# Thresholded attention and a bilinear FFN: weight conversion steps and the first ffn portions in another order within the opening slots

## The chip, the cores and the metric

One core of a Trainium2 chip runs the whole program. The metric is the device time of one execution in microseconds; several executions are timed, and the median is given. One more execution is recorded by the hardware profiler, which gives the trace that the tables below are read from.

## The reference

Inputs are q, k and v of shape (8, 8, 576, 64) (batch, heads, sequence, head size), a scalar tau, and weights w_a, w_b (512 x 1536) and w_out (1536 x 512) that come as 64-bit floats. For each of the 64 heads:

```
scores = q @ k.T / 8
scores = where(scores >= max(scores, row) - tau, scores, -1e9)
attn   = exp(scores - max);  attn /= sum(attn) + 1e-9
x      = attn @ v            # heads side by side: 4608 x 512
out    = ((x @ w_a) * (x @ w_b)) @ w_out
```

## The kernel before, in words

**Units and slots.** Two heads form a pair (32 pairs). A unit is 128 query rows of both heads of a pair; the last 64 rows of both heads form a shorter one. The main loop (L756) runs over slots g. Slot g issues unit g's scores and weights (mask and softmax), the transposition of the weights of unit g-1, the product with v of a unit some slots back, and a portion of the ffn as a filler. At the end each engine is held to exactly the order in which the code issued its instructions (`keep_order`, L38), so the order of the calls in a slot is the order of each engine's queue.

**One unit.** `scores` (L314): TensorE writes two PSUM tiles `sc`; VectorE takes row maxima `mx` (L332); GpSimd makes `bias` (L334) and `thr` (L336) of them while weights are being converted. `weigh` (L353): ScalarE takes exp (L364), then VectorE's mask (L367) compares with `thr`, multiplies, and sums the row. `reciprocal` (L372) adds 1e-9 to the sums, on ScalarE (L376) or VectorE (L378), and takes the reciprocal on VectorE (L380).

**Two ways to transpose.** For the first eight units (g < BY_PE) ScalarE builds two diagonal matrices of the reciprocals (`diagonals`, L393), and TensorE multiplies the weights by them in the next slot (`turn_pe`, L406 and L412), ScalarE and VectorE copying the result out (L408, L414). Two slots later `weighted_unit` (L499) multiplies by v (L479), ScalarE and VectorE join the two halves (L468, L469), and GpSimd copies the halves crosswise into a second tile `xS` (`exchange`, L489). From unit 8 on ScalarE normalises (L386), VectorE transposes in blocks (L433), and SP's queue writes to DRAM and reads back (L441, L464).

**Weight conversion.** The 64-bit weights come as 36 pieces, each of 128 x 512 numbers as pairs of 32-bit words. `load_weights` (L193) keeps up to four rooms called `raw` filled, and from slot 3 four more in `sums_u32`; a piece's room comes free with its sign step. A piece n of slot g is turned into 32-bit floats in five steps: `convert_first` (two ScalarE instructions, L225 and L226), `convert_clamp` (GpSimd, L232), and in slot g+1 `convert_sign` (VectorE, L238), `convert_shift` (VectorE, L246) and `convert_add` (GpSimd, L251). The table `early` gives slots 0 to 3 two pieces each, slots 4 to 9 three each, slots 10 to 14 two each. The ffn may use a piece only once it is counted in `state["converted"]`.

**The ffn.** `ffn` (L553) is a generator: every step of it issues a few matmuls. For a tile of 128 hidden columns it runs eight steps with w_a (L578), ScalarE copies the product out (L584), then eight with w_b, and VectorE multiplies the two (L586). It gives control back with nothing done (`yield 0, 0, 0`, L566) while the pieces or rows that it needs are missing. `advance` (L699) takes steps until the columns owed are used up:

```
advance((PORTIONS[2] if g > BY_PE else sum(PORTIONS[:3])) * pace)   # L826
advance(PORTIONS[3] * pace)                                         # L827
```

In slots 0 to 8 the whole portion stands at these two lines, at the slot's end; later slots spend parts of it at L787, L799, L826 and L827. The first block of rows exists from slot 5 on, and each of slots 5 to 8 issues 11 or 12 steps.

**PSUM.** Four buffers (`banks`, L125) of two banks each serve scores, turned weights, products and ffn tiles in turn.

**The order in a slot of the start, before:** scores and maxima; join and exchange of the unit two back; signs of all pieces of the slot before, then their shifts, then their adds (the last piece's first); new loads; exp and masks; the transposition of unit g-1; the first steps and clamp of this slot's first piece; add of 1e-9 (on ScalarE) and reciprocal; diagonals; the first steps and clamps of the other pieces; loads; the ffn's portion.

Of the kernel before, what the change touches and what calls it, by code (L numbers as in the profile page):

```python
# [23 lines left out]
BY_PE = 8  # L24
# [8 lines left out]
PORTIONS = (0.3, 0.35, 0.15, 0.2)  # L33
# [18 lines left out]
def kernel(  # L52
# [38 lines left out]
    nc = tc.nc  # L91
# [40 lines left out]
    loaded = {}  # L132
# [38 lines left out]
    for f in range(NG):  # L171
        for c in range(HP):
            for dst, w in ((wa_sb, w_a), (wb_sb, w_b)):
                src = []
                for r in range(2):
                    chunks = [(2 * c + e) % HP * 2 + (r + (c >= HP // 2)) % 2 for e in range(2)]
                    cols = slice(f * CW + r * CH, f * CW + (r + 1) * CH)
                    rows = w[:, cols].bitcast(U32).rearrange("(k p) f -> p k f", p=D)
# [3 lines left out]
        pieces.append((wo_sb[:, F, :], [w_out[F * P:(F + 1) * P, :].bitcast(U32)]))  # L182
    NPIECES = len(pieces)
    raws, stages, extra, taken = {}, {}, [], {}
    state = {"loaded": 0, "converted": 0, "rows": 0, "sums": False, "through": 0, "over": False}


    NSUM = NF // 2 * 3 * CH
# [46 lines left out]
    def convert_sign(n):  # L235
        if n in stages:
            low, hi = stages[n].bitcast(U32), raws.pop(n)[:, :, 1]
            nc.vector.scalar_tensor_tensor(out=low, in0=hi, scalar=0x80000000, in1=low,  # L238
                                           op0=ALU.bitwise_and, op1=ALU.bitwise_or)
            if n in taken:  # L240
                extra.append(taken.pop(n))

    def convert_shift(n):
        if n in stages:
            top = pieces[n][0].bitcast(U32)
            nc.vector.tensor_scalar(top, top, 3, None, op0=ALU.logical_shift_left)  # L246

    def convert_add(n):
        if n in stages:
            top, low = pieces[n][0].bitcast(I32), stages.pop(n).bitcast(I32)  # L250
            nc.gpsimd.tensor_tensor(top, top, low, op=ALU.add)  # L251
            state["converted"] += 1


    scalars = const.tile([P, 8], FP32, name="scalars")
# [55 lines left out]
    def prep_copy(mT, tp):  # L311
        nc.vector.tensor_copy(mT.rearrange("p (c k) -> p c k", c=2), tp)  # L312
# [40 lines left out]
    def weigh(i, u):  # L353

        sc, thr, bias, mx, biased = scored.pop((i, u))
        n = len(sc)
        sums = small.tile([P, 2], FP32, tag="sums", name="sums")
        ws = rooms_of(i, u)
        sb = [s.rearrange("p c (n e) -> p c n e", e=Q) for s in sc]
        wb = [w.rearrange("p (c n) e -> p c n e", c=2) for w in ws]  # L360
        for j in range(n):
            if not biased:
                nc.scalar.activation(bias[:, j:j + 1], mx[:, j:j + 1], AF.Copy, scale=e_nscale)
            nc.scalar.activation(wb[j], sb[j], AF.Exp, bias=bias[:, j:j + 1], scale=e_scale)  # L364
        for j in range(n):
            wv = wb[j]
            nc.vector.scalar_tensor_tensor(  # L367
                out=wv, in0=sb[j], scalar=thr[:, j:j + 1], in1=wv,
                op0=ALU.is_ge, op1=ALU.mult, accum_out=sums[:, j:j + 1])
        weights[i, u] = (ws, sums)  # L370

    def reciprocal(i, u, engine):  # L372
        ws, sums = weights[i, u]
        n = len(ws)
        if engine is nc.scalar:
            nc.scalar.activation(sums[:, 0:n], sums[:, 0:n], AF.Copy, bias=1e-9)  # L376
        else:
            nc.vector.tensor_scalar_add(sums[:, 0:n], sums[:, 0:n], 1e-9)  # L378
        rcp = small.tile([P, 2], FP32, tag="rcp", name="rcp")
        nc.vector.reciprocal(rcp[:, 0:n], sums[:, 0:n])  # L380
        weights[i, u] = (ws, rcp)

    def normalise(i, u):
        ws, rcp = weights[i, u]
        for j, w in enumerate(ws):
            nc.scalar.activation(w, w, AF.Copy, scale=rcp[:, j:j + 1])  # L386
# [35 lines left out]
    def width(i, h):  # L422
        return (HALF, HALF, TAIL)[h] if i < HP else (HALF, HALF + TAIL)[h]
# [269 lines left out]
    def cost():  # L693

        return BLOCK_COLS - (NF // 2 * CH if state["sums"] else 0)
# [3 lines left out]
    def advance(cols):  # L699
        running["owed"] += cols  # L700
        while running["owed"] > 0:
            if running["ffn"] is None:
                if not blocks:
                    running["owed"] = 0.0
                    return
                running["ffn"] = ffn(*blocks.pop(0))
                running["left"] = cost()
            step, rest, whole = next(running["ffn"], (None, 0, 0))
            if step == 0:
                running["owed"] = 0.0  # L710
                return
            if step is None:
                running["ffn"] = None
                state["through"] += 1
            else:
                running["owed"] -= step
                running["left"] -= step
                running["done"] = running["done"] + step if rest else 0
                running["rest"] = rest
                running["room"] = min(ROOM, whole // 2)  # L720
# [9 lines left out]
    def backlog():  # L730
        return len(blocks) * cost() + (running["left"] if running["ffn"] is not None else 0)
# [16 lines left out]
    for name in ("q", "k"):  # L748
        prep_copy(*prep_pe(0, name))
    early = {}  # L750
    n = 0
    for g in range(NPIECES):
        size = min(3 if 4 <= g < 10 else 2, NPIECES - n)
# [1 line left out]
        n += size  # L755
    for g in range(len(units) + PV_LAG):  # L756
        written = len(pending)
        here = g < len(units)
        converting = bool(early.get(g)) or bool(early.get(g - 1))
        if here:  # L760
            i, u = units[g]
            scores(i, u)
        turn_back()
        exchange_blocks()
        pace = (PACE if g > BY_PE else PACE_EARLY) * BLOCK_COLS
        if g > BY_PE:
            pace = min(pace, backlog() / (min([a for a in arrivals if a > g] + [len(units) + PV_LAG + 1]) - g))
        pace += (NSLOT + 1) // 2 * S / (NT + 1) + CATCH_UP * max(backlog() - BLOCK_COLS, 0)
        if 2 <= g < BY_PE + 2:
            weighted_unit(*units[g - 2])  # L770
            running["owed"] -= (NSLOT + 1) // 2 * P
        if g < 3:
            prep_copy(*prep_pe(g + 1, "q"))
        for n in early.get(g - 1, []):
            convert_sign(n)
        for n in early.get(g - 1, []):
            convert_shift(n)
        for n in early.get(g - 1, [])[-1:] + early.get(g - 1, [])[:-1]:
            convert_add(n)
        if g == 3:  # L780
            for c in range(0, NSUM - 2 * CW + 1, 2 * CW):
                extra.append(sums_u32[:, c:c + 2 * CW].rearrange("p (f w) -> p f w", w=2))
        load_weights(RAWS)
        if g > BY_PE and g <= len(units):
            turn_blocks(*units[g - 1])
        if g > BY_PE:
            advance(PORTIONS[0] * pace)  # L787
        if here:
            weigh(i, u)
        if 0 < g <= BY_PE:  # L790
            turn_pe(*units[g - 1])
        if g < 3:
            prep_copy(*prep_pe(g + 1, "k"))
        for p in range(HP, NPR):
            for name, d in (("q", 2), ("k", 1)):
                if g == first[p] - d:
                    prep(p, name)
        if g > BY_PE:
            advance(PORTIONS[1] * pace)  # L799
            n = g - PV_LAG  # L800
            if BY_PE <= n < len(units) and part(*units[n]):
                make_room()
                weighted(*part(*units[n]))
                running["owed"] -= (NSLOT + 1) // 2 * width(*part(*units[n]))
        for n in early.get(g, [])[:1]:
            convert_first(n)
            convert_clamp(n)
        if here:
            reciprocal(i, u, nc.scalar if converting else nc.vector)
        if here and g < BY_PE:  # L810
            diagonals(i, u)
        elif here:
            normalise(i, u)
        for n in early.get(g, [])[1:]:
            convert_first(n)
            convert_clamp(n)
        load_weights(RAWS)
        for p in range(HP, NPR):
            for name, d in (("q", 4), ("k", 3)):
                if g == first[p] - d:  # L820
                    load(p, name)
        for p in range(1, NPR):
            if g == first[p] - 1:
                load_v(p)
        store(written)
        advance((PORTIONS[2] if g > BY_PE else sum(PORTIONS[:3])) * pace)  # L826
        advance(PORTIONS[3] * pace)  # L827

        if not converting and not state["sums"]:
            state["slots"] = state.get("slots", 0) + 1  # L830
            for n in {1: (0,), 2: (1,), 3: (2,)}.get(state["slots"], ()):
                for z in range(2):
                    weight_sums(n, z)
            if state["slots"] >= 3 and state["through"]:
                for z in range(2):
                    weight_sums(3, z)
                state["sums"] = True
# [38 lines left out]
```

## Time and profile before

| | us |
|---|---|
| median of 7 runs | 1482.24 (1478.39 to 1483.79) |
| the profiled execution's own time | 1483.91 |
| its span, first to last instruction | 1482.0 |
| TensorE matmul busy | 1423.6 (96%) |
| VectorE busy | 927.0 (63%) |
| ScalarE busy | 670.4 (45%) |
| GpSimd busy | 361.3 (24%) |

Busy time is the time that an engine's instructions cover; matmuls are pipelined, so a busy TensorE is not one at its peak. The mean granted TensorE clock is 0.995 of full speed. In the tables PE is TensorE's matmul, PEld its weight load, DVE VectorE, ACT ScalarE, POOL GpSimd and SP the engine whose queue issues the DMAs. A row of a timeline gives start, duration, engine, line, operation, output and input, the number of instructions merged, and in brackets the idle time of the engine ahead of it and what ended that. Row sums of idle time by what ended it are called waits.

### The profile page before, as it was taken

How to read it: one execution, taken by the hardware profiler on the slowest of the kernel's cores; microseconds unless marked ns; L12 is line 12 of the kernel's file. 1: busy time of each engine (PE TensorE's matmuls, PEld its weight loads, DVE VectorE, ACT ScalarE, POOL GpSimd, SP SyncE). 2: the span in 40 equal slices, each digit the busy share in tenths (PEclk: the TensorE clock that was granted, in tenths of full speed). 3: DMA queues.
4: the chain of work that ended last, by engine and by line, in shares of the span. 5: the costliest groups of instructions: out<-in, count | busy, mean ns of one | idle time of the engine just before them, and what ended most of it. 6: DMA issues, size and time to landing. Idle time of an engine off the chain costs nothing.

```text
span 1482.0 us, 57127 instructions
## 1 busy us (share of the span) xinstructions
PE 1423.6 (96%) x25344; PEld 1197.3 (81%) x25344; DVE 927.0 (63%) x2068; ACT 670.4 (45%) x1213; POOL 361.3 (24%) x563
## 2 busy tenths in 40 slices
PE   5778999999999999999999999999999999999998
PEld 4667587898779798898888788889888898888886
DVE  5767677778657776776655766577756775622212
ACT  4866355545445554544443544455444454411010
POOL 3876512204030312122121203030404040310000
PEclk9999999999999999999999999999999999999999
DMA  9956888889868876797556876588756986530000
GB/s 202 213 171 168 170 167 182 195 155 191 201 129 182 188 173 151 167 188 170 110 133 132 181 165 150 119 187 180 158 145 135 192 175 158 136 90 16 2 17 16
DMA packets 624582, 220.75 MB, mean 149 GB/s; under 512 B 542928, under 2 KB 612048, under 8 KB 624336
## 3 DMA queue, kind: packets, MB, share of 16 engines
q1 hardware_dynamic: 621968, 216.52, 66.6%
q8 instruction: 199, 3.26, 0.9%
q10 hardware_dynamic: 2368, 0.59, 0.2%
q14 instruction: 47, 0.39, 0.1%
HBM read 127.40 MB, written 89.65 MB: 146 GB/s over the span
## 4 chain that ended last, share of the span: by engine, by line
PE 87%; DVE 5%; DMA 2%; ACT 2%; SPq 1%; issue 1%; POOL 1%; ACTq 0%; DVEq 0%; POOLq 0%
PE pab L578 46%; PE po L621 19%; PE pv L479 10%; PE sc L325 10%; PE po L665 1%; DMA swap<-tw 1%; DVE tw L433 1%; DVE tw L367 1%; DVE mx L332 1%; DVE low L238 1%; ACT tw L364 1%; SPq L151 0%; DMA sums_u<-in_moe_w_a_dram 0%; SPq L206 0%; DMA sums_u<-in_k_dram 0%
## 5 line engine op out<-in xcount | busy, mean ns | idle before, releaser
L332 DVE TENSOR_REDUCE mx<-sc 128x1 f32<-128x576 f32 x288 | 205.3, 750 | 129.3 <-PE sc L325 118.5
L578 PE MATMUL pab<-xS,wa_sb 64*64 64x256 f32 (+1 forms) x3584 | 271.8, 371 | 0.9 <-POOL xS L489 0.9
L578 PE MATMUL pab<-xS,wb_sb 64*64 64x256 f32 (+1 forms) x3584 | 268.0, 372 | 0.2 <-issue 0.2
L325 PE MATMUL sc<-kT,qT 64*64 64x288 f32 x2304 | 242.0, 411 | 21.9 <-DVE kT L312 7.8
L590 POOL TENSOR_TENSOR h<-h 128x256 f32<-128x256 f32 x168 | 117.5, 732 | 543.4 <-PE po L621 540.3
L578 PE MATMUL pab<-xT,wb_sb 64*64 64x256 f32 (+1 forms) x3200 | 236.2, 370 | 5.6 <-DVE h L586 4.1
L578 PE MATMUL pab<-xT,wa_sb 64*64 64x256 f32 (+1 forms) x3200 | 235.8, 368 | 5.3 <-POOL thr L336 2.1
L621 PE MATMUL po<-wo_sb,h 64*64 64x256 f32 x3264 | 240.4, 376 | 0.0
L386 ACT ACTIVATE tw<-tw,rcp 128x576 f32<-128x576 f32 x244 | 176.4, 769 | 131.4 <-DVE rcp L380 131.3
L364 ACT ACTIVATE tw<-sc,bias,scalars 128x576 f32<-128x576 f32 x260 | 214.9, 832 | 41.8 <-POOL bias L334 26.4
L367 DVE SCALAR_TENSOR_TENSOR tw<-sc,thr,tw 128x576 f32<-128x576 f32 x260 | 203.9, 803 | 23.9 <-ACT tw L364 22.9
L578 PEld LDWEIGHTS pab<-xS,wa_sb 64*64 64x64 f32 x3584 | 192.3, 133 | 31.6 <-POOL xS L489 5.2
L578 PEld LDWEIGHTS pab<-xS,wb_sb 64*64 64x64 f32 x3584 | 194.2, 134 | 24.9 <-issue 0.8
L621 PEld LDWEIGHTS po<-wo_sb,h 64*64 64x64 f32 x3264 | 174.7, 132 | 26.3
L578 PEld LDWEIGHTS pab<-xT,wa_sb 64*64 64x64 f32 x3200 | 169.1, 133 | 30.3 <-DVE kept L469 4.3
L578 PEld LDWEIGHTS pab<-xT,wb_sb 64*64 64x64 f32 x3200 | 170.4, 134 | 27.8 <-DVE h L586 4.5
L479 PE MATMUL pv<-wT,vm 64*64 64x320 f32 (+3 forms) x2592 | 185.9, 379 | 5.0 <-ACT h L584 3.2
L325 PEld LDWEIGHTS sc<-kT,qT 64*64 64x64 f32 x2304 | 142.4, 134 | 55.3 <-issue 16.8
L621 PE MATMUL po<-sums_u,h 64*64 64x256 f32 x2448 | 180.8, 376 | 0.0
L433 DVE STREAM_TRANSPOSE tw<-tw 128x576 f32<-128x576 f32 x240 | 171.7, 753 | 0.2 <-ACT tw L386 0.2
L586 DVE TENSOR_TENSOR h<-h,pab 128x512 f32<-128x512 f32 (+1 forms) x112 | 73.4, 656 | 148.8 <-PE pab L578 140.9
L479 PEld LDWEIGHTS pv<-wT,vm 64*64 64x64 f32 x2592 | 140.0, 134 | 28.4 <-ACT h L584 4.3
(85 smaller groups left out, 1238.0 us busy)
## 6 DMA issues: line engine op xcount, KB each, us to landing
swap<-tw SPq DMA_DIRECT2D x240, 288.0 KB, 5.3
wT<-swap SPq DMA_DIRECT2D x28, 1440.0 KB, 7.6
wT<-swap SPq DMA_DIRECT2D x32, 1152.0 KB, 6.4
vm<-in_v_dram SPq DMA_DIRECT2D x32, 288.0 KB, 4.8
qT<-in_q_dram SPq DMA_DIRECT2D x112, 72.0 KB, 3.7
kT<-in_k_dram SPq DMA_DIRECT2D x112, 72.0 KB, 4.5
swap<-wt SPq DMA_DIRECT2D x112, 72.0 KB, 2.8
out_dram<-kept SPq DMA_DIRECT2D x30, 256.0 KB, 4.5
```

The costliest lines, as they stand in the source:

```text
L238: nc.vector.scalar_tensor_tensor(out=low, in0=hi, scalar=0x80000000, in1=low, op0=ALU.bitwise_and, op1=ALU.bitwise_or)
L325: nc.tensor.matmul(sc[j if u < NT else 0][to, c], qT[r, q0:q0 + D], kT[r, c * SH:(c + 1) * SH], start=True, stop=True)
L332: nc.vector.tensor_reduce(mx[:, c], sc[j], axis=AX.XY, op=ALU.max)
L364: nc.scalar.activation(wb[j], sb[j], AF.Exp, bias=bias[:, j:j + 1], scale=e_scale)
L367: nc.vector.scalar_tensor_tensor(out=wv, in0=sb[j], scalar=thr[:, j:j + 1], in1=wv, op0=ALU.is_ge, op1=ALU.mult, accum_out=sums[:, j:j + 1])
L386: nc.scalar.activation(w, w, AF.Copy, scale=rcp[:, j:j + 1])
L433: nc.vector.transpose(w, w)
L479: nc.tensor.matmul(pv[j * D:(j + 1) * D, r], vm[rows, k0], wT[rows, k0], start=(s == (NT if j == r else 0)), stop=(s == NT - 1))
L578: nc.tensor.matmul(pab[c * D:(c + 1) * D, r], w[rows, f // n, k, fs + c * D:fs + (c + 1) * D], moving, start=(k == 0), stop=(k == H - 1))
L586: nc.vector.tensor_tensor(ht, ht, pab, op=ALU.mult)
L590: (nc.vector if state["over"] else nc.gpsimd).tensor_tensor(*a, **kw)
L621: nc.tensor.matmul(po[c * D:(c + 1) * D, r, y], ht[rows, t0:t0 + D], other[rows, f], start=(f == 0), stop=(f == NF // 2 - 1))
```

## The change

- The steps that finish a piece (sign, shift, add) are put together in `convert_rest(g, k)`, which handles piece k of the slot before. Piece 0 stays where all of them were, pieces 1 and 2 follow the reciprocal and the diagonals or the normalising; in slots 0 to 8 the ffn's portion stands between pieces 1 and 2.
- In slots 0 to 7 the add of 1e-9 and the reciprocal directly follow the masks, both on VectorE.
- In slots 0 to 8 the ffn's whole portion is issued ahead of the first steps of this slot's second and third piece. In later slots it stays at the end.
- A piece that is added counts as converted from the start of the next slot on.

```diff
@@ -182,7 +182,7 @@
         pieces.append((wo_sb[:, F, :], [w_out[F * P:(F + 1) * P, :].bitcast(U32)]))
     NPIECES = len(pieces)
     raws, stages, extra, taken = {}, {}, [], {}
-    state = {"loaded": 0, "converted": 0, "rows": 0, "sums": False, "through": 0, "over": False}
+    state = {"loaded": 0, "added": 0, "converted": 0, "rows": 0, "sums": False, "through": 0, "over": False}
 
 
     NSUM = NF // 2 * 3 * CH
@@ -249,7 +249,7 @@
         if n in stages:
             top, low = pieces[n][0].bitcast(I32), stages.pop(n).bitcast(I32)
             nc.gpsimd.tensor_tensor(top, top, low, op=ALU.add)
-            state["converted"] += 1
+            state["added"] += 1
 
 
     scalars = const.tile([P, 8], FP32, name="scalars")
@@ -748,6 +748,14 @@
     for name in ("q", "k"):
         prep_copy(*prep_pe(0, name))
     early = {}
+
+    def convert_rest(g, k):
+
+        for n in early.get(g - 1, [])[k:k + 1]:
+            convert_sign(n)
+            convert_shift(n)
+            convert_add(n)
+
     n = 0
     for g in range(NPIECES):
         size = min(3 if 4 <= g < 10 else 2, NPIECES - n)
@@ -755,6 +763,7 @@
         n += size
     for g in range(len(units) + PV_LAG):
         written = len(pending)
+        state["converted"] = state["added"]
         here = g < len(units)
         converting = bool(early.get(g)) or bool(early.get(g - 1))
         if here:
@@ -771,12 +780,7 @@
             running["owed"] -= (NSLOT + 1) // 2 * P
         if g < 3:
             prep_copy(*prep_pe(g + 1, "q"))
-        for n in early.get(g - 1, []):
-            convert_sign(n)
-        for n in early.get(g - 1, []):
-            convert_shift(n)
-        for n in early.get(g - 1, [])[-1:] + early.get(g - 1, [])[:-1]:
-            convert_add(n)
+        convert_rest(g, 0)
         if g == 3:
             for c in range(0, NSUM - 2 * CW + 1, 2 * CW):
                 extra.append(sums_u32[:, c:c + 2 * CW].rearrange("p (f w) -> p f w", w=2))
@@ -787,6 +791,8 @@
             advance(PORTIONS[0] * pace)
         if here:
             weigh(i, u)
+        if here and g < BY_PE:
+            reciprocal(i, u, nc.vector)
         if 0 < g <= BY_PE:
             turn_pe(*units[g - 1])
         if g < 3:
@@ -805,12 +811,15 @@
         for n in early.get(g, [])[:1]:
             convert_first(n)
             convert_clamp(n)
-        if here:
-            reciprocal(i, u, nc.scalar if converting else nc.vector)
         if here and g < BY_PE:
             diagonals(i, u)
         elif here:
+            reciprocal(i, u, nc.scalar if converting else nc.vector)
             normalise(i, u)
+        convert_rest(g, 1)
+        if g <= BY_PE:
+            advance(pace)
+        convert_rest(g, 2)
         for n in early.get(g, [])[1:]:
             convert_first(n)
             convert_clamp(n)
@@ -823,8 +832,9 @@
             if g == first[p] - 1:
                 load_v(p)
         store(written)
-        advance((PORTIONS[2] if g > BY_PE else sum(PORTIONS[:3])) * pace)
-        advance(PORTIONS[3] * pace)
+        if g > BY_PE:
+            advance(PORTIONS[2] * pace)
+            advance(PORTIONS[3] * pace)
 
         if not converting and not state["sums"]:
             state["slots"] = state.get("slots", 0) + 1
```

## The prediction

> **What bounds the kernel now.** I read the page's busy row first, then busy time by stretches, then the engines' timelines from 40 to 110 us, then the waits of PE. The busy row says PE 96%, which hides where its idle time lies. So I cut the span at the starts of slots 0, 4, 10 and 16 (a slot starts with its first score matmul: 11.25, 40.21, 101.72, 154.08 us); columns are PE, PEld, DVE, ACT, POOL, clock, DMA share, GB/s:
>
> ```profile
> 11.25:40.21 28.96, 22.11 (x233) 16.68 (x233) 21.97 (x48) 19.03 (x38) 15.11 (x27) 1.00 1.03 196
> 40.21:101.72 61.51, 44.02 (x940) 37.85 (x942) 41.55 (x99) 45.64 (x91) 49.87 (x67) 0.97 0.79 198
> 101.72:154.08 52.36, 42.85 (x942) 36.49 (x938) 42.01 (x87) 33.35 (x58) 35.92 (x43) 0.97 0.67 165
> 154.08:200.00 45.92, 44.98 (x623) 30.67 (x619) 28.36 (x62) 18.37 (x31) 20.52 (x27) 0.96 0.85 172
> 200.00:1482.00 1282.00, 1267.50 (x22617) 1073.73 (x22609) 791.15 (x1769) 552.76 (x998) 239.21 (x394) 1.00 0.66 144
> ```
>
> From 154 us on PE idles 15.4 us in 1328: it sets the end, and whatever the first 16 slots save or lose moves the end by as much. Those slots hold 33.9 us of idle PE (6.85 + 17.5 + 9.5), and all of the change lies in them. In slots 4 to 9 POOL is the busiest engine (49.87 of 61.5), in 10 to 15 PE and DVE. One slot's chain, slot 8 into 9:
>
> ```profile
> 81.64 0.30 POOL L336 TENSOR_SCALAR thr<-mx,scalars 128x2 f32<-128x2 f32 x1
> 82.32 1.32 POOL L489 COPY xS<-xT 64x128 f32<-64x128 f32 x2 [0.39 <-DVE xT L469]
> 85.34 2.53 POOL L251 TENSOR_TENSOR wb_sb<-wb_sb,low 128x512 int32<-128x512 int32 x2 [1.70 <-DVE wb_sb L246]
> 87.82 1.28 POOL L251 TENSOR_TENSOR wa_sb<-wa_sb,low 128x512 int32<-128x512 int32 x1
> ...
> 90.95 0.55 POOL L334 TENSOR_SCALAR bias<-mx,scalars 128x1 f32<-128x1 f32 x2
> ```
> ```profile
> 90.18 0.65 ACT L226 ACTIVATE low<-raw 128x512 f32<-128x512 uint32 x1
> 90.74 0.35 ACT L584 COPY h<-pab 128x256 f32<-128x256 f32 x1
> ```
> ```profile
> 91.14 1.20 PE L479 MATMUL pv<-wT,vm 64*64 64x128 f32 x34 [1.60 <-ACT h L584]
> ...
> 97.83 1.99 PE L578 MATMUL pab<-xT,wb_sb 64*64 64x128 f32 x32 [2.68 <-DVE h L586]
> 99.58 1.88 PE L578 MATMUL pab<-xS,wb_sb 64*64 64x128 f32 x32
> ```
>
> The reader is to see three things. POOL waits 1.70 us, because its first add comes after all three signs and shifts on DVE. The softmax bias of the next slot stands behind POOL's adds and clamps. And ACT's copy of a finished ffn product stands behind four conversions, though PE had that product ready at about 87.3; PE's next matmul lacks the PSUM buffer meanwhile.
>
> **The change, part by part.** Slots 0 to 3. In slot 2 the two signs and two shifts fill DVE from 30.26 to 32.23, ahead of the masks (L367) and of the k copy (L312) that slot 3's scores wait for. The second pair, 0.98, now follows that copy and lies in the 1.22 us in which DVE waits for the next scores. The add (0.28, L378) and reciprocal (0.17) come ahead of the copy: +0.45. Net -0.53 in slots 1 and 2, +0.45 in slot 0, which has no pair to finish. Slot 3 ends with ACT's turn copies; its bias now waits for the late add and clamp (pair done about 1.0 after the scores start, 1.25 + 0.6 more; bias at 2.8 instead of 2.1): +0.6. Sum 0.0.
>
> SP's queue: a piece's room is freed by its sign. Counting rooms (four raw, four sums, the latter from slot 3), piece 5 loads only after the sign that now ends slot 1, at about 27.5 instead of 23.61; 1.25 us of issue and 5.6 of landing (the median; 9.7 the longest) bring it to 34.4, and ACT takes it at about 34.5 (35.35 before). Piece 7 likewise: 42.3 against 42.24. Cover gone: 0 to 4 us, I take +0.5. The v loads queued behind have a slot to spare. From slot 4 on loads run 8 us or more ahead.
>
> Slots 4 to 8. Three PE waits end with the late copy (L584): 1.63 at 60.11, 0.86 at 79.29, 1.60 at 91.14. The copy now precedes the four conversions (4 x 0.56), so these 4.1 us go. The conversions wait for PE's ffn instead, but the tile is done within 0.1 us of the diagonals in my walk. What is late next is POOL: from bias to bias its slots took 9.27, 9.83, 9.73, 10.49 and 12.82 us (slots 5 to 9, 52.14 in all). Unhindered it needs 0.55 + 0.30 + 0.7 to 1.3 + 3 x 1.25 + 3 x 0.6 = 7.1 to 7.7. I walked slots 5 to 9 in the new order with these durations: the first add follows the exchange at once, since one sign and shift (0.98) fit beside it; the second follows the pair behind the masks; the third follows a pair behind DVE's ffn product. Slot 5, from its first bias: DVE's join ends at 0.5, pair 1 at 1.5, the masks (exp has just finished) at 2.95, add and reciprocal at 3.45, turn copy at 3.75, pair 2 at 4.75, pair 3 at 5.7. POOL: bias and thr, which the first sign holds, to 1.45; exchange 2.15; add 1 to 3.4; clamp 1 to 4.05; add 2 from 4.75 to 6.0; add 3 to 7.25; two clamps to 8.45, the next bias. The five slots so: 8.5, 8.7, 9.6 (add 3 waits 0.8 for the ffn product), 9.1, 9.3, mean 9.0.
>
> The moved pairs then run beside adds, which no row shows. Nearest rows: the exchange took 1.32 beside signs (82.32) and 0.62 beside masks (45.99), so about half speed; and thr took 1.54 beside signs (71.79), 0.30 without. For a pair beside an add that is 0 to 0.98; I take 0.5 by the exchange, the nearer form, in four of five slots: mean 9.4. Gain 5 x (10.4 - 9.4) = 5.1; with slot 4, where one pair leaves the masks' front, 5.5. Ends: 3.6 (both pairs stop POOL, 9.7 a slot) and 13.6 (7.7 a slot).
>
> [...]
>
> Slot 9. At 97.83 PE waits 2.68 for a product behind three pairs and two transposes, then issues 64 matmuls in 3.5 us, where 104.00 and 104.88 took 1.75. Two pairs (1.96) leave the front. The wait is in POOL's period already; of the slow stretch's 1.7 us I take 1.0, bounds 0 and 1.7.
>
> [...]
>
> Slots 10 to 15. Order there changes on DVE and POOL alone. PE waits ended by DVE: 1.53 (109.25), 1.38 (116.63), 3.71 (144.94), 0.96 (152.25). One pair less ahead (two in slot 10) takes at most 1.53 + 0.98 + 0.98 + 0.96 = 4.45. The second add now starts a pair behind the reciprocal, and the bias of the next slot stands behind it: reciprocal + 1.1 + 1.25 + 0.6 = 3.0 against 2.8 by normalise, conversion and clamp. 0.2 x 5 = 1.0 lost. Net -3.5.
>
> Held pieces. A piece counts one slot later. Slot 7's ffn then has 14 pieces and needs 16: it stops after 9 of 11 k-steps, and 2 x 0.22 = +0.45 comes later, on a full PE. Later gates have pieces to spare (by counting steps, 34 in slot 15, where output begins).
>
> Sum: 0.0 + 0.5 - 5.5 - 1.0 - 3.5 + 0.45 = -9.05. The profiled execution took 1483.91 (span 1482.0 and 1.9 around it), 1.67 over the median of the seven runs, 1482.24. So 1474.9 on the profiled one's scale, and **1473** on the median's.
>
> **Rivals.** (1) Part of it is taken back: POOL is stopped by the pairs and the loads of slots 2 and 3 come late. Then slots 4 to 8 give 3.6, slots 10 to 15 half (1.7), the slow stretch stays, loads cost 2: -5.3 + 2 + 0.45 = -2.9, 1479.3. For it: thr's 1.54. Against: the exchange. (2) Slower: POOL's in-order queue. The last add waits for a sign behind DVE's ffn product, which waits for PE; product, pair, add and two clamps (0.35 + 0.98 + 1.25 + 1.2 = 3.8) then stand between PE's last ffn matmul and the next bias. Place: slots 5 to 15. It decides as soon as bias to bias exceeds the 10.4 of now; with two adds held up so (5.05) against 3.8 a slot has 1.25 more than my 9.4 and ends at 10.65 before any stop of POOL; 0.5 for that makes it 11.15, +0.7 in 11 slots, less the 2 us that earlier copies still give: +6, 1488. For it: my slot 7 already has POOL waiting 1.4 us this way. Against: the ffn of slots 5, 6 and 8 completes no second-weight tile late in the slot. (3) More than forecast: PE keeps pace with 7.7 us of POOL work; the 13.6 end less 3 for the waits that stay, with 1.7 and 4.45, and the +0.95 of loads and held steps: -16, 1466. (4) It does not act: buffers are handed out otherwise, PE waits for a mask instead of a copy: 1482.
>
> **How the numbers follow.** Forecast 0.60 (1468 to 1478), (1) 0.17, (2) 0.10, (3) 0.08, (4) 0.05. The range must leave out 0.2 at most: it reaches from 1466 over forecast and (1) to 1481, leaving out (2), (4) and the outer part of (3). 0.2% is 3 us, about what a measurement here can tell from no change. Faster by more: forecast, (3) and half of (1), 0.77. Within: half of (1) and (4), 0.13. Slower: 0.10.
>
> **What would show it.** Right: no PE wait on ACT's h copy in slots 5 to 9; POOL's bias-to-bias near 9.4; the idle before the first add gone from 1.70 to under 0.5; slot 10's scores 7 us earlier; slot 16's 9 earlier; from there on the same lengths. Wrong: adds above 1.7 us beside signs, bias more than 4 us behind its scores, an ACT wait on a weight load in slots 2 and 3, or the gain of slot 16 missing at the end, which would mean that PE doesn't set it.

## The result and the profile after

The changed kernel takes 1475.84 us (median of 22 runs, 1472.35 to 1481.24) against 1482.33 of before in the same comparison: ratio 0.9961, 95% interval 0.9952 to 0.9970, so 5.8 us less (4.4 to 7.1; the two medians lie 6.5 apart). Its profiled execution took 1476.51 (span 1474.5), 7.4 less than that of before (1483.91). The forecast was 1473.

These are the stretches of the changed kernel, cut at its own starts of slots 0, 4, 10 and 16, with the columns of the prediction's first fence:

```profile
10.95:39.40 28.45, 22.13 (x233) 17.03 (x233) 22.70 (x49) 18.08 (x34) 14.87 (x27) 1.00 1.06 198
39.40:97.07 57.67, 44.73 (x933) 39.08 (x935) 49.24 (x100) 43.14 (x84) 46.10 (x65) 0.94 0.82 195
97.07:148.91 51.84, 44.03 (x958) 37.39 (x954) 45.68 (x89) 34.49 (x60) 34.04 (x44) 0.97 0.75 191
148.91:194.80 45.89, 43.59 (x612) 29.75 (x608) 27.34 (x62) 18.30 (x30) 21.72 (x28) 0.99 0.82 168
194.80:1474.50 1279.70, 1265.20 (x22618) 1088.67 (x22609) 792.41 (x1771) 551.97 (x998) 238.59 (x394) 1.00 0.66 144
```

Slots 4 to 9 are 3.8 us shorter (61.51 to 57.67), and DVE now has more busy time there than POOL: 49.24, where it had 41.55. It runs about as many rows (x100 for x99); some of them take longer (the four shifts of slots 0 to 15 that meet an add of GpSimd take 1.50 each, without an add 0.42 is the median). Slots 10 to 15 lost 0.5 us (52.36 to 51.84), slots 0 to 3 0.5.

The same chain as in the prediction, slot 8 into 9, on GpSimd:

```profile
83.18 0.63 POOL L489 COPY xS<-xT 64x128 f32<-64x128 f32 x2
83.90 1.28 POOL L251 TENSOR_TENSOR wb_sb<-wb_sb,low 128x512 int32<-128x512 int32 x1
...
87.58 1.65 POOL L251 TENSOR_TENSOR wa_sb<-wa_sb,low 128x512 int32<-128x512 int32 x1 [1.17 <-DVE wa_sb L246]
89.60 1.29 POOL L251 TENSOR_TENSOR wb_sb<-wb_sb,low 128x512 int32<-128x512 int32 x1 [0.37 <-DVE wb_sb L246]
...
92.03 1.23 POOL L334 TENSOR_SCALAR bias<-mx,scalars 128x1 f32<-128x1 f32 x2
```

ScalarE, where the copy of the ffn product (L584) now stands ahead of four conversions:

```profile
88.10 0.37 ACT L584 COPY h<-pab 128x256 f32<-128x256 f32 x1
88.37 0.68 ACT L225 ACTIVATE wb_sb<-sums_u 128x512 f32<-128x512 f32 x1
```

TensorE, slots 8 and 9:

```profile
84.44 1.91 PE L578 MATMUL pab<-xT,wa_sb 64*64 64x128 f32 x32 [2.92 <-DVE tw L367]
...
89.74 1.14 PE L479 MATMUL pv<-wT,vm 64*64 64x128 f32 x33
...
95.05 1.10 PE L578 MATMUL pab<-xT,wb_sb 64*64 64x128 f32 x32 [1.33 <-DVE tw L367]
```

The reader is to see that each wait which the change was to remove is gone: the first add follows the exchange at once (the 1.70 has no successor), and the product with v no longer waits 1.60 for ScalarE (89.74 has no bracket). But GpSimd now waits 1.17 and 0.37 between its adds, and from bias to bias it still takes 9.89 (82.14 to 92.03). TensorE waits for VectorE's masks instead, 2.92 us, because the bias comes late: 5.3 us behind the scores of slot 8, where it was 3.2. One such wait stands in each of slots 5 to 8 (0.78, 1.59, 1.58 and 2.92 us); before, no wait there was ended by the masks.

### The profile page after: what moved, and what is told of

It is laid out like the page before. It is cut to its first block, busy times and chain, and to the rows that moved or that the text cites. A ratio compares the mean times of both kernels' runs of the same rounds, so it can differ in the third digit from the quotient of the medians.

```text
span 1474.5 us, 57127 instructions
## 1 busy us (share of the span) xinstructions
PE 1421.8 (96%) x25344; PEld 1213.8 (82%) x25344; DVE 939.4 (64%) x2076; ACT 667.3 (45%) x1205; POOL 356.0 (24%) x563
## 4 chain that ended last, share of the span: by engine, by line
PE 85%; DVE 6%; DMA 3%; ACT 2%; SPq 2%; issue 2%; POOL 1%; DVEq 0%; ACTq 0%; POOLq 0%
PE pab L578 46%; PE po L621 19%; PE sc L325 10%; PE pv L479 9%; DVE mx L332 1%; DVE tw L367 1%; DMA swap<-tw 1%; DVE low L238 1%; SPq L143 1%; DVE tw L433 1%; PE po L665 1%; DMA raw<-in_moe_w_a_dram 0%; ACT tw L364 0%; DMA sums_u<-in_moe_w_a_dram 0%; SPq L441 0%
## 5 line engine op out<-in xcount | busy, mean ns | idle before, releaser
L621 PEld LDWEIGHTS po<-wo_sb,h 64*64 64x64 f32 x3264 | 177.9, 132 | 23.4
L578 PEld LDWEIGHTS pab<-xT,wb_sb 64*64 64x64 f32 x3200 | 172.1, 133 | 24.8 <-DVE h L586 3.2
L325 PEld LDWEIGHTS sc<-kT,qT 64*64 64x64 f32 x2304 | 145.8, 134 | 50.7 <-issue 15.7
L479 PEld LDWEIGHTS pv<-wT,vm 64*64 64x64 f32 x2592 | 144.1, 134 | 22.6 <-DVE h L586 2.8
```

Source lines behind the costliest of these rows:

```text
L325: nc.tensor.matmul(sc[j if u < NT else 0][to, c], qT[r, q0:q0 + D], kT[r, c * SH:(c + 1) * SH], start=True, stop=True)
L479: nc.tensor.matmul(pv[j * D:(j + 1) * D, r], vm[rows, k0], wT[rows, k0], start=(s == (NT if j == r else 0)), stop=(s == NT - 1))
L578: nc.tensor.matmul(pab[c * D:(c + 1) * D, r], w[rows, f // n, k, fs + c * D:fs + (c + 1) * D], moving, start=(k == 0), stop=(k == H - 1))
L621: nc.tensor.matmul(po[c * D:(c + 1) * D, r, y], ht[rows, t0:t0 + D], other[rows, f], start=(f == 0), stop=(f == NF // 2 - 1))
```

## The experiments

Each ratio is to the kernel before, run on the same chip in the same comparison. "us" is the ratio times 1482. Lengths of stretches come from one profiled execution of each kernel.

| kernel | ratio (95%) | us | slots 0-3 | 4-8 | 9 | 10-11 | 12-14 | 15 |
|---|---|---|---|---|---|---|---|---|
| before | 1 | 0 | 28.96 | 48.13 | 13.38 | 18.24 | 24.98 | 9.14 |
| changed | 0.9961 (0.9952 to 0.9970) | -5.8 | 28.45 | 49.37 | 8.30 | 19.53 | 22.05 | 10.26 |
| changed_again | 0.9962 (0.9945 to 0.9979) | -5.6 | 28.16 | 48.02 | 9.81 | 21.24 | 22.26 | 10.26 |
| split_only | 0.9998 (0.9986 to 1.0011) | -0.3 | 29.17 | 49.85 | 11.24 | 21.70 | 22.81 | 8.85 |
| ffn_ahead_only | 0.9986 (0.9972 to 1.0001) | -2.1 | 30.54 | 48.38 | 9.95 | 18.66 | 24.96 | 9.56 |
| sums_early_only | 1.0076 (1.0060 to 1.0093) | +11.3 | 36.33 | 52.39 | 12.89 | 18.52 | 24.95 | 10.00 |
| count_later_only | 0.9971 (0.9959 to 0.9984) | -4.3 | 28.96 | 46.34 | 12.96 | 18.37 | 22.31 | 9.19 |
| hold_1 | 0.9977 (0.9964 to 0.9990) | -3.4 | 28.39 | 50.99 | 13.36 | 18.02 | 22.32 | 10.75 |
| hold_4 | 0.9985 (0.9974 to 0.9997) | -2.2 | 32.37 | 46.61 | 11.48 | 20.52 | 23.37 | 9.40 |
| count_and_ffn | 0.9935 (0.9917 to 0.9952) | -9.6 | 32.86 | 48.67 | 10.07 | 18.36 | 22.34 | 9.18 |
| no_sums_early | 0.9965 (0.9952 to 0.9979) | -5.2 | 27.70 | 51.20 | 8.37 | 20.62 | 22.47 | 8.89 |
| no_split | 0.9998 (0.9987 to 1.0008) | -0.3 | 34.95 | 46.11 | 14.24 | 19.02 | 22.30 | 9.78 |
| early_rcp_no_add | 0.9965 (0.9950 to 0.9980) | -5.2 | 29.41 | 47.87 | 13.09 | 18.01 | 22.29 | 10.74 |
| pairs_together | 0.9958 (0.9942 to 0.9973) | -6.2 | 28.09 | 48.83 | 8.20 | 19.30 | 22.72 | 10.02 |

One caution for the table: slots 0 to 3 of before, hold_4 and hold_1 are the same program and took 28.96, 32.37 and 28.39 us in their one profile each, so a difference of 3 or 4 us there carries nothing by itself. Slots 12 to 14 repeat to 0.05 us among the kernels without the split that share TensorE's order there; the two profiles of the changed kernel differ by 0.21.

### The four parts alone

Each of these four is the kernel before with one part of the change.

**split_only.** Pieces 1 and 2 are finished behind the diagonals or the normalising.

```diff
-        for n in early.get(g - 1, []):
-            convert_sign(n)
...
+        convert_rest(g, 0)
...
+        convert_rest(g, 1)
+        convert_rest(g, 2)
```

> The kernel before with one part of the change: pairs of sign and shift (and their add) of pieces 1 and 2 behind the reciprocal; ffn portion, reciprocal and counting as before. Theory A (the gain is slot 9, where fewer pairs stand ahead of DVE's ffn product, and pairs beside adds gain nothing in slots 4 to 8): faster by 4 to 6 us, slot 9 shorter than 9.5 us (13.4 before), bias to bias of slots 5 to 8 within 0.4 of before's 9.8. Theory B (the gain is the early ffn copy): within 2 us of before, slot 9 above 12 us.

Measured: 0.9998, no difference. The time is as theory B expected, but slot 9 took 11.24, which neither theory allows (under 9.5, above 12), so neither is shown by this run.

**ffn_ahead_only.** In slots 0 to 8 the ffn's portion goes ahead of the late conversions.

```diff
+        if g <= BY_PE:
+            advance(pace)
         for n in early.get(g, [])[1:]:
             convert_first(n)
```

> The kernel before with one part of the change: in slots 0 to 8 the ffn portion ahead of the first steps of pieces 1 and 2; all signs, shifts and adds in front as before. Theory A: faster by at most 3 us, since POOL's ring sets slots 5 to 8, whoever is early on PE. Theory B: faster by 4 to 7 us, the three waits of PE on the copy (4.1 us) gone and slot 9 shorter by over 2 us.

Measured: 0.9986, 2.1 us less, with an interval that just takes in no change. Slot 9 falls from 13.38 to 9.95. The time keeps to theory A's bound of 3 us, and theory B's 4 to 7 us did not come, though slot 9 shrank as B asked.

**sums_early_only.** Add and reciprocal at once behind the masks in slots 0 to 7.

```diff
+        if here and g < BY_PE:
+            reciprocal(i, u, nc.vector)
         if 0 < g <= BY_PE:
             turn_pe(*units[g - 1])
```

> The kernel before with one part of the change: in slots 0 to 7 the add of 1e-9 and the reciprocal on VectorE right behind the masks. Theory A and B: no change, within 1 us; 0.45 us more on VectorE in slot 0, 1 and 2 ahead of the k copy, less wait of the diagonals. A third theory (this part carries the gain by freeing ScalarE): faster by over 3 us.

Measured: 11.3 us slower, the largest effect of any part, and against the change; none of the three theories expected it. VectorE and then GpSimd of this kernel just behind the masks of slot 1, and what TensorE does next:

```profile
25.86 1.11 DVE L378 TENSOR_SCALAR sums<-sums 128x2 f32<-128x2 f32 x1
27.00 0.17 DVE L380 RECIPROCAL rcp<-sums 128x2 f32<-128x2 f32 x1
```
```profile
25.65 1.28 POOL L251 TENSOR_TENSOR wa_sb<-wa_sb,low 128x512 int32<-128x512 int32 x1
```
```profile
28.07 2.21 PE L325 MATMUL sc<-kT,qT 64*64 64x288 f32 x16 [1.39 <-DVE kT L312]
```

An addition on two numbers a row takes 1.11 us and ends at 26.97, 0.04 behind the end of GpSimd's add at 26.93. With no add of GpSimd under way it takes 0.17 to 0.28 (five of the eight in the changed kernel). The copy of k stands behind it, and the next scores behind that; they then run at half pace (2.21 instead of 1.22). This adds to the loss: from 23 us to the start of slot 10 the granted clock is at half for 24.8 us in this profile, and for 3.4 us in that of before.

**count_later_only.** A piece counts as converted one slot later.

```diff
-            state["converted"] += 1
+            state["added"] += 1
...
+        state["converted"] = state["added"]
```

> The kernel before with one part of the change: a piece counts from the next slot on, so that two ffn k-steps of slot 7 come in slot 8 and TensorE's whole later order moves by two steps. By the prediction's term: 0.45 us slower at most. Rival: the other order of TensorE behind slot 16 is what gave the changed kernel 2.3 us there; then faster by 1.5 to 3 us, most of it behind 160 us.

Measured: 0.9971, 4.3 us less. The part that the forecast booked as a loss of 0.45 is the largest gain of the four. The rival expected 1.5 to 3 us, most of it behind 160 us; the gain is larger, and what the profile shows of it lies ahead of slot 16 (see below).

### Parts together, and parts left out

**count_and_ffn** joins later counting and the ffn ahead, without split and early sums.

```diff
+        state["converted"] = state["added"]
...
+        if g <= BY_PE:
+            advance(pace)
         for n in early.get(g, [])[1:]:
             convert_first(n)
```

> The kernel before with two parts: the later counting and the ffn portion ahead of the late conversions; no split, reciprocal as before. If the parts add up: 4.3 + 2 = 6 us faster than before, as much as the whole change, which then owes nothing to the split and the early sums. Rival (both remove the same waits of slots 8 and 9): 4 us or less.

Measured: 1472.35 against 1481.67, 0.9935. It beats both kernels: 9.6 us less than before, and by medians about 3.5 less than the changed one (the two intervals only touch, that of changed_again overlaps, and they were not run on one chip). It is more than the 6 us expected if the parts add up, and the rival's 4 us or less is refuted.

**no_sums_early** is the changed kernel with the reciprocal back in its old place.

```diff
-        if here and g < BY_PE:
-            reciprocal(i, u, nc.vector)
...
+        if here:
+            reciprocal(i, u, nc.scalar if converting else nc.vector)
```

> The changed kernel without one part: the add of 1e-9 (on ScalarE again) and the reciprocal stand where they stood. Theory L (VectorE's short add waits for a GpSimd add that runs beside it; in the changed kernel the split has moved GpSimd's adds away, so that the early sums cost little there): within 1.5 us of the changed kernel, 5 to 8 us faster than before. Rival (the early sums carry some of the change's gain, their own loss being of the old order alone): 2 us or more slower than the changed kernel, under 4.5 us faster than before.

**no_split** is the changed kernel with all pairs ahead of the masks again.

```diff
-        convert_rest(g, 0)
+        for n in early.get(g - 1, []):
+            convert_sign(n)
...
-        convert_rest(g, 1)
...
-        convert_rest(g, 2)
```

> The changed kernel without one part: all signs, shifts and adds in front again, early sums, early ffn and later counting kept. Theory L: VectorE's add of 1e-9 stands beside GpSimd's second add again and takes 1.1 us instead of 0.3 in slots 1 to 3, TensorE goes to half pace there; slot 4 starts 5 to 8 us later than in the changed kernel, the whole is 3 to 8 us slower than before. Rival (early sums alone lost time for some other reason that the other parts remove): faster than before by 3 us or more.

Measured, on the chip of count_and_ffn: 0.9965 and 0.9998. The first keeps to theory L. The second does not: L expected 3 to 8 us slower than before, and it is as fast as before, though its slots 0 to 3 are 6.5 us longer than the changed kernel's, as L asked (5 to 8). So neither part gains by itself. Without early sums the split costs 4.4 us (0.9965 against 0.9935, intervals that touch; on before alone it costs nothing, 0.9998); with them it saves 5.5 (0.9961 against 0.9998, on different chips). What the rows show for the saving is that it moves GpSimd's second add away from the small addition, which takes 0.17 to 0.45 in the changed kernel and 1.11 to 1.27 in five of its seven meetings in no_split; in the other two GpSimd's add was nearly over (0.30 and 0.44). In sums_early_only, where the addition has the same place, it takes 1.11 to 1.27 in five of seven too, and 0.29 and 0.44 in the others. Early sums without the split cost 9.3 (0.9998 against 0.9935). The two together are repair and damage.

### Is it the lock, or the early reciprocal?

"Lock" means here that an instruction of VectorE is not over until an add of GpSimd, which runs beside it, is over, as with the addition above (26.97 behind 26.93).

**early_rcp_no_add** is count_and_ffn with the reciprocal of slots 0 to 7 at once behind the masks, and without the addition of 1e-9 in these slots.

```diff
-        if engine is nc.scalar:
+        if engine is None:
+            pass
+        elif engine is nc.scalar:
...
+        if here and g < BY_PE:
+            reciprocal(i, u, None)
```

> The kernel before with the later counting and the ffn part ahead of the late conversions, and with the reciprocal of slots 0 to 7 on VectorE at once behind the masks, but without the addition of 1e-9 (left out in those slots). Pairs of converting steps stay together as before. Theory of the lock (the small addition waits out GpSimd's addition, 1.11 us against 0.17 to 0.28 alone; the reciprocal itself is not the price): 8 to 12 us faster than before, like the later counting and the ffn part alone (0.9935). Rival (any small instruction on VectorE ahead of the copies of turned weights is held up, or the reciprocal is locked out as the addition was): within 2 us of before, like the changed kernel without the split (0.9998), with the reciprocal of slots 2 and 3 at 0.8 us or more.

Measured: 0.9965, between the two. VectorE, GpSimd and TensorE in the same place as above:

```profile
26.39 0.17 DVE L382 RECIPROCAL rcp<-sums 128x2 f32<-128x2 f32 x1
```
```profile
26.21 1.27 POOL L251 TENSOR_TENSOR wa_sb<-wa_sb,low 128x512 int32<-128x512 int32 x1
```
```profile
27.46 1.22 PE L325 MATMUL sc<-kT,qT 64*64 64x288 f32 x16 [1.02 <-DVE kT L312]
```

The reciprocal runs beside the add at its usual 0.17 in all seven meetings of slots 1 to 7, these scores keep full pace, and slots 0 to 3 take 29.41, where the two kernels with the addition in this place take 36.33 and 34.95 (count_and_ffn, with neither, took 32.86 in its one profile). By these ratios the addition costs 4.9 us of the 9.3 (0.9998 to 0.9965; two chips, but the intervals lie apart). The other 4.4 (0.9965 to 0.9935, different chips, intervals that just overlap) is not explained. In the one profile slot 9 is 3.0 us longer than in count_and_ffn, of which 1.6 is half pace behind a wait of the same 3.08; the rest stays open. The forecast of 8 to 12 for the lock was too high, the rival's "within 2 us of before" is refuted.

### What sets GpSimd's period?

**pairs_together** is the changed kernel with pieces 1 and 2 both signed and shifted ahead of the ffn's portion, and then both added.

```diff
-        for n in early.get(g - 1, [])[k:k + 1]:
+        some = early.get(g - 1, [])[0:1] if k == 0 else early.get(g - 1, [])[1:]
+        for n in some:
             convert_sign(n)
+        for n in some:
             convert_shift(n)
+        for n in some:
             convert_add(n)
...
-        convert_rest(g, 2)
```

> The changed kernel with the signs and shifts of the second and third piece together behind the diagonals, ahead of the ffn part, and GpSimd's two additions behind them. Theory of the lock (GpSimd's last addition waits 0.97 for a pair that itself waited for the addition before it): the 0.97 before the last addition goes, bias to bias on GpSimd falls from 10.14 to 9.7 or less in slots 4 to 9, and the time is 0 to 3 us below the changed kernel's. Rival (the period is set elsewhere, by VectorE's masks and copies): bias to bias stays at 10.0 or more and the time within 1 us of the changed kernel's, or above it where VectorE's copies stand behind the pairs.

Measured: 0.9958, beside 0.9962 of the changed kernel on the same chip: no difference. GpSimd's last two adds of slot 8 and the next bias:

```profile
87.61 1.39 POOL L251 TENSOR_TENSOR wa_sb<-wa_sb,low 128x512 int32<-128x512 int32 x1 [1.76 <-DVE wa_sb L246]
88.96 1.28 POOL L251 TENSOR_TENSOR wb_sb<-wb_sb,low 128x512 int32<-128x512 int32 x1
...
91.38 1.23 POOL L334 TENSOR_SCALAR bias<-mx,scalars 128x1 f32<-128x1 f32 x2
```

The wait between the two adds is gone as expected, and is paid ahead of the first of them (1.76 for 1.17). From 51.83 to 102.04 the mean of five periods is 10.04 us; the changed kernel has 10.14, and 10.20 in its second profile. The theory expected 9.7 or less, so it falls for this question, and the rival holds. What the profile shows instead is a ring through three engines. In slot 7 of this kernel the bias starts at 71.39, the masks end at 74.46, both pairs at 77.60, both adds at 79.98, two clamps at 81.7, and the next bias starts there. In either order pairs 2 and 3 stand between the masks, which need the bias, and the adds, which the next bias stands behind.

Three pairs of kernels differ by the split alone; without it all pairs stand ahead of the masks. The mean of the three periods from the bias of slot 5 to that of slot 8 is 9.61 us in before and 10.62 in split_only, 9.78 in count_and_ffn and 10.71 in no_sums_early, 9.66 in no_split and 10.07 in changed (10.20 in its second profile). So the split lengthens the period by 0.4 to 1.0 us. That it does so by closing this ring was read off the traces; no run tests it.

### Why does later counting gain?

**hold_4** and **hold_1** are the kernel before with four contraction steps, or one, less of the ffn owed in slot 7.

```diff
+        if g == 7:
+            running["owed"] -= 4 * P
```

> The kernel before with the ffn of slot 7 cut by four k-steps (512 columns less are owed), which come later; nothing else. Theory P (the later counting gains by where the ffn's tiles then end in the slots, not by holding steps): anything between 3 us faster and 4 us slower. Rival (fewer ffn steps in slot 7 are what gains): 4 to 9 us faster.

> The kernel before with one contraction step less of the ffn part owed in slot 7, and nothing else; TensorE's order becomes that of the later counting but for some twenty instructions. Theory of alignment (what the later counting won is that slot 7 no longer ends on a half-open tile of the ffn that keeps one of four PSUM buffers): 3 to 5 us faster than before. Rival (the later counting wins by something else, or holding any work does it): within 1.5 us of before, as with four steps less (0.9985).

Measured: 0.9985 and 0.9977. Holding four steps gives 2.2 us, within theory P's range and short of the rival's 4 to 9. Holding one gives 3.4, as much as the later counting within the intervals and within the 3 to 5 that were expected. But the place that I named for it was wrong, so that number came out by luck. In hold_1 slot 7 still ends on an open tile, and slot 8's scores still wait for the buffer:

```profile
76.04 0.40 PE L578 MATMUL pab<-xT,wa_sb 64*64 64x128 f32 x8
76.26 1.14 PE L325 MATMUL sc<-kT,qT 64*64 64x288 f32 x8
78.58 0.70 PE L325 MATMUL sc<-kT,qT 64*64 64x288 f32 x4 [1.19 <-ACT h L584]
...
144.11 1.22 PE L325 MATMUL sc<-kT,qT 64*64 64x288 f32 x16 [0.82 <-DVE tw L367]
```

(This profiled execution took 1482.41, five over the kernel's median, with slots 8 and 9 partly at half pace, 16 matmuls of L406 in 3.79 at 82.58 where the changed kernel has 2.05; its stretches 4 to 8 and 9 are not used.) What hold_1 and the later counting share is the order of TensorE's work from slot 9 on, and with it slots 12 to 14: 22.32 and 22.31 us. The same three slots take 22.34, 22.30 and 22.29 in the three other kernels with that order and without the split, and 24.98, 24.96 and 24.95 in before, ffn_ahead_only and sums_early_only. That is 2.65 us, the same in eight profiles. TensorE at the end of slots 12 and 14, in before:

```profile
126.55 0.66 PE L578 MATMUL pab<-xT,wb_sb 64*64 64x256 f32 x8
127.29 1.28 PE L325 MATMUL sc<-kT,qT 64*64 64x288 f32 x14
...
139.27 1.96 PE L578 MATMUL pab<-xT,wb_sb 64*64 64x256 f32 x30
144.94 1.59 PE L325 MATMUL sc<-kT,qT 64*64 64x288 f32 x16 [3.71 <-DVE tw L367]
```

And in count_later_only:

```profile
122.66 1.96 PE L578 MATMUL pab<-xS,wa_sb 64*64 64x256 f32 x32
124.38 1.43 PE L325 MATMUL sc<-kT,qT 64*64 64x288 f32 x12
...
138.64 0.63 PE L578 MATMUL pab<-xS,wb_sb 64*64 64x256 f32 x4
140.09 1.22 PE L325 MATMUL sc<-kT,qT 64*64 64x288 f32 x16 [0.83 <-DVE tw L367]
```

Before starts a tile with eight matmuls at the end of slot 12 and has its ffn work done at 141.2 in slot 14; then it waits 3.71 for the masks. In the later counting the tile begins in the next slot, everything lies further back, and slot 14 has work up to 139.3; the wait is 0.83. In before slots 13 and 14 hold 88 and 64 ffn matmuls, in the later counting 64 and 104. So the filler stands where TensorE would wait. By the start of slot 16 the kernels with later counting or one step held have also done 24 output matmuls instead of 16, which is 0.9 us more (16 take 1.9). Together 3.6, which covers hold_1 and all but 0.7 of the later counting's 4.3.

**changed_again** is the changed kernel once more, beside the last three.

> The changed kernel as it is, on the same chip as the three others: 0.995 to 0.997 of before by either theory.

Measured: 0.9962.

## Why the prediction was right, and where it was wrong

The sign came out and the size nearly, 1473 forecast against 1475.84. But several steps failed, with opposite signs, so the nearness of the total is partly luck. Slot 10 starts 4.7 us earlier, not 7, and slot 16 5.2 us earlier, not 9.

- **Slots 0 to 3: 0.0, and late loads +0.5.** Measured -0.5, and no wait on a weight load in slots 2 and 3. Right, within what these slots vary. What held it right was the split, by luck: I priced the addition at 0.28, and in no_split it takes 1.11.
- **Slots 4 to 8: -5.5.** Failed. Measured +1.2 (-0.1 in the second profile). The three waits for the late copy went, as forecast, with no such wait left in slots 5 to 9. The failed step is "For a pair beside an add that is 0 to 0.98; I take 0.5 by the exchange": the period is 10.14, not 9.4, and 10.43 before. Over slots 5 to 9, which that sum was made for, the gain is 1.4 us (1.15 in the second profile), not 5.1, and all of it is slot 9's: 9.27, 9.83, 9.73, 10.49 and 12.82 became 10.02, 10.10, 10.10, 9.89 and 10.61. In slots 5 to 7 the split, which was to gain 1.0 a slot, costs 0.4 to 1.0 (three pairs of kernels, above).
- **Slot 9: -1.0.** Failed in size: measured -5.1 (-3.6). I had put the 2.68 wait into GpSimd's period; the period hardly moved, and the wait fell to 1.33 all the same, without the half pace behind it. Slots 4 to 9 together: forecast -6.5, measured -3.8 and -3.7.
- **Slots 10 to 15: -3.5.** Measured -0.5 (+1.4). It is a sum that I had not seen: later counting alone gives -2.5 there (49.87 in count_later_only), and the split takes 1 to 2 back (51.84, 53.76, 51.98 and 52.04 in the four profiles with split and later counting, against 49.87 to 51.10 in the five without the split that share TensorE's order).
- **Held pieces: +0.45 "on a full PE".** Failed, in sign. Two steps held are not two steps lost: TensorE isn't full in slots 12 to 14, and the held work fills waits there. Worth -4.3 alone, -3.6 of it seen in its place.
- **Slot 16 on: same lengths.** 1327.9 before and 1325.6 after, but over all fourteen profiles the rest takes 1320.3 to 1327.9 with no order in it; 0.9 of the difference is output matmuls done earlier. With that scatter one profile can't tell whether a gain of 5 us in the first 16 slots arrives at the end; the clearest sign that it does is sums_early_only, whose slot 16 starts 12.0 us later and whose time is 11.3 us longer.
- **The rivals.** The sign that I named for trouble did appear: the bias is 4.9 to 5.3 us behind the scores in slots 5 to 8, where 4 was the bound. The slower rival asked for a period over the old one; that did not come in the mean of the five, though slots 5, 6 and 7 each grew by 0.3 to 0.8, and "part of it is taken back" is nearest in time. The condition of rival (4), PE waiting for a mask instead of a copy, is what slots 5 to 8 show.

The failed period, item by item, in slot 5, which the prediction walked. First VectorE, then GpSimd of the changed kernel; the bias starts at 51.92:

```profile
55.05 0.45 DVE L378 TENSOR_SCALAR sums<-sums 128x2 f32<-128x2 f32 x1
...
55.80 0.85 DVE L238 SCALAR_TENSOR_TENSOR low<-sums_u,low 128x512 uint32<-128x512 uint32 x1
56.58 0.41 DVE L246 TENSOR_SCALAR wb_sb<-wb_sb 128x512 uint32<-128x512 uint32 x1
56.91 0.68 DVE L238 SCALAR_TENSOR_TENSOR low<-sums_u,low 128x512 uint32<-128x512 uint32 x1
57.51 1.50 DVE L246 TENSOR_SCALAR wa_sb<-wa_sb 128x512 uint32<-128x512 uint32 x1
```
```profile
57.07 1.66 POOL L251 TENSOR_TENSOR wb_sb<-wb_sb,low 128x512 int32<-128x512 int32 x1 [0.96 <-DVE wb_sb L246]
59.10 1.26 POOL L251 TENSOR_TENSOR wa_sb<-wa_sb,low 128x512 int32<-128x512 int32 x1 [0.37 <-DVE wa_sb L246]
...
60.91 1.05 POOL L232 TENSOR_SCALAR wb_sb<-wb_sb 128x512 f32<-128x512 f32 x1
```

The walk had the second add from 4.75 to 6.0, the third to 7.25 and the next bias at 8.45. Measured from 51.92: 5.15, 6.81, 8.44 and 10.02. The 1.57 are, but for 0.01: 0.40 mostly because addition and sign took 0.45 and 0.85; 0.41 because the add began beside a sign and took 1.66; 0.37 because the third piece's shift waited until that add was over (57.51 to 59.01; alone 0.42); 0.38 in the clamps, of which the last ran beside a sign (1.05 for 0.6). I had seen that GpSimd is held up by signs. I had not seen that VectorE is held up by GpSimd's adds, and the 0.5 that I took in four slots of five, 0.4 in the mean, is 1.14 (10.14 against the walk's 9.0). The profile of before did show a case, behind the stretch that I read: at 189.90 an L378 addition took 1.04 us and ended 0.03 behind a subtraction of GpSimd (L550, 189.09 to 190.91), where most such additions took 0.11 to 0.17.

Over slots 0 to 15, beside an add of GpSimd, shifts took 1.50 for 0.42 (changed kernel) and the small addition 1.11 to 1.27 (sums_early_only) for 0.17 to 0.28 (changed kernel), while row maxima (0.74 for 0.75), reciprocals (0.17 for 0.17) and masks (0.81 for 0.82, all three in before) hardly changed.

## What to carry to other kernels

When an instruction is moved on VectorE, look at what GpSimd runs at its new place: a small operation can be held by large ones of the other engine, and a chain stands behind it. Here VectorE's addition on 2 numbers a row took 1.11 to 1.27 us beside GpSimd's adds and 0.17 to 0.28 without, and GpSimd's `thr`, also on 2, 1.54 beside VectorE's signs and 0.30 without. Work that fills waits is worth what the waits at its place are worth; holding it a slot may be a gain, so look for waits late in the stretch before pricing a delay as a loss. Where a change has several parts, run each part alone and leave each one out: here the total came near the forecast while two parts cancelled each other, and half of the change measured faster than the whole, by intervals that only touch.

## What the runs showed of the hardware that was not expected

- Whether VectorE waits for GpSimd's add went by the kind of operation and not by size: an addition on 2 numbers a row waited as long as a shift on 512 (1.11 and 1.50 beside adds of 1.28 and 1.66), and a reciprocal on 2 did not wait (0.17).
- The pace of TensorE behind a wait is not a function of the wait. In the result's fence 32 matmuls took 1.91 us behind 2.92 of waiting; the repetition of the same program, TensorE in the same slot:

```profile
84.37 1.10 PE L578 MATMUL pab<-xT,wa_sb 64*64 64x128 f32 x32 [2.93 <-DVE tw L367]
```

  The same 3.08 us is followed by 1.99 in early_rcp_no_add and by 1.10 in count_and_ffn, and in sums_early_only half pace followed a wait of 1.39. The granted clock tells why. In the fourteen profiles it is 1 or 0.5, every stretch at half lasts 3.41 us or twice that (but for the last one, which runs past the end), and every stretch at full between them is a whole multiple of 3.41 us. So in these profiles the clock changes on a grid of 3.41 us only, which lies differently in each execution (a line of it at 84.57 in one of the changed kernel's, at 82.83 and 86.25 in the other). These are two stretches of the changed kernel's grid, then two of its repetition's, with the columns of the result's first fence:

```profile
81.16:84.57 3.41, 0.49 (x8) 0.24 (x12) 2.29 (x5) 1.95 (x4) 3.20 (x7) 1.00 0.78 247
84.57:87.98 3.41, 3.41 (x68) 3.41 (x70) 2.34 (x7) 3.18 (x7) 1.62 (x3) 0.50 0.05 18
...
79.42:82.83 3.41, 2.02 (x19) 1.66 (x18) 2.95 (x5) 0.28 (x2) 3.41 (x6) 1.00 0.76 202
82.83:86.25 3.42, 1.88 (x68) 1.88 (x72) 1.76 (x5) 3.42 (x7) 2.58 (x5) 1.00 0.41 140
```

  In the first the wait of 2.92 fills one stretch of the grid, with 0.49 us of matmuls, and the next is at half. In the repetition the wait of 2.93 is divided over two, with 2.02 and 1.88, and the clock stays full. So the length of one wait does not decide it. From 25 to 175 us, over the fourteen profiles, each stretch at full clock with under 1.45 us of matmuls was followed by half clock (0.74 and 0.72 in before, 0.49 and 1.33 in the changed kernel), and of those with over 1.9 only one was (2.23, in hold_1). How much of the 4 us by which slots 0 to 3 of one program differ (28.39 to 32.37) goes with this was not shown.
